# Two 128-step chunks in place of the third 256-step window, and a new order of all work, in an RWKV recurrence followed by an MLP mixer

## The chip, the cores and the metric

The kernel runs on one core of a Trainium2 chip. Its engines work side by side, each through its own list of instructions: TensorE (PE) multiplies matrices, VectorE (DVE), ScalarE (ACT) and GpSimd (POOL) work elementwise, and SyncE (SP) issues transfers; POOL and ACT issue some too. The metric is the device time of one execution in microseconds (us). Several runs of the kernel before give its median.

## The reference

Inputs are r, k, v of 4 batches x 8 heads x 768 steps x 48, a decay w and a bonus u of 8 heads x 48, and four mixer weights, all f32. Per head, a 48x48 state runs over the steps:

```python
for t in range(S):
    cur = np.einsum('bhd,bhe->bhde', u[None] * kt, vt)
    y[:, :, t] = np.einsum('bhd,bhde->bhe', rt, state + cur)
    state = w[None, :, :, None] * state + np.einsum('bhd,bhe->bhde', kt, vt)
```

So each output has a part from the state of earlier steps and a part from its own step, `cur`. The outputs, as x of 4 x 768 x 384, go through a mixer: `u = x + (relu(x^T w_tok1) w_tok2)^T`, over the 768 steps with 256 hidden, and `out = u + relu(u w_ch1) w_ch2`, over the 384 columns with 1536 hidden.

## The kernel before

**Chunks and windows.** A batch's 768 steps are six chunks of 128. In an ordinary chunk (`unit`, from line 801) k and r of 128 steps x 384 columns are scaled by powers of the decay (`kr`), transposed by PE (`tr_ps` or `trk`, copied to SBUF as `rkb`, `rka`), and multiplied head by head into 128x128 scores (`at_ps`); DVE masks these to earlier steps (`AT0` and `AT1`, for the even and the odd heads); PE multiplies the masked scores by v and adds the state's part (`y_ps`). The state is carried from chunk to chunk: key-value products (`kv_ps`), masked and decayed to `S0`. For the own step, the product of k, r and u is summed over a head (`pr`, `ad_ps`, `adg`) and weighs v (`yd`).

Batch 0 is worked in *windows* of 256 steps (`window`, from line 527; its loads and products `pairs`, from line 626). One load then brings two neighbouring steps to each partition (`win`, 384 KB, against 192 KB of a chunk's `kt`, `rt`, `vt`). Even and odd steps are worked apart, so a window has two sets of scores of 64x128 for each half, masked by `mask2`, and outputs of 32 small matmuls (`y_ps<-vb,AT`, line 750). Its own-step part, `ydb`, is put in place by four PE matmuls against `place` (line 760), and the sum leaves PSUM by a plain copy into `x_b0`. `two_steps` (line 451) says which loads are windows. r of an ordinary chunk in batches 0 and 1 is loaded for two chunks at once as well.

**The mixer.** `h_ps` (x by `wtok1`; batch 0 in three groups: chunks 0 to 2, then 3 and 4, then 5), relu to `h1r`, then back by `wtok2` (`hx_ps`, `hT_ps`) to `u_sb`, transposed to `uT`; `z_ps` (up by `wch`, 12 blocks), relu to `zr`, `h_ps` (down by `wch`), plus u into `osb`, and stores.

**What sets the order.** All work is cut into tasks with names; `Plan.run` (lines 151 to 198) emits them in the sequence of the table ORDER. Each engine runs its own tasks in that sequence, and waits for what they need. BUFS says which buffer each tile takes, ENGINES which engine does a task that several could do. WAITS (line 130) ties a few transfers to the start of an earlier one. The weights are fetched by POOL, in its list between its products (`load_weights`, line 501): `wtok1`, `wtok2`, two parts of `wch1`, and three of `wch2`. FILL puts matmuls on a constant tile (`warm`) ahead of some tasks, with results that nobody reads; NWARM more of them are tasks of their own (`keep_warm`, line 1209).

All engine calls go through a helper, so nearly all rows of the profile have one line, L239; they are told apart by tiles.

Of the kernel before, what the change touches and what calls it, by code (L numbers as in the profile page):

```python
# [21 lines left out]
    0, 3, 7, 22, 2, 19, 17, 51, 1, 38, 42, 5, 21, 52, 4, 12, 6, 867, 868, 23, 20, 54, 15, 55, 24, 8, 18, 9, 16, 45,  # L22
    27, 58, 29, 120, 28, 13, 43, 118, 30, 53, 14, 121, 10, 149, 57, 869, 870, 871, 872, 873, 874, 875, 876, 877, 878,
    123, 119, 150, 879, 122, 124, 147, 56, 25, 44, 152, 125, 46, 148, 177, 61, 26, 126, 132, 36, 153, 135, 11, 39,
    134, 127, 151, 129, 41, 59, 178, 136, 133, 154, 140, 181, 179, 141, 60, 161, 184, 155, 143, 180, 128, 162, 156,
    164, 158, 70, 144, 111, 182, 157, 137, 169, 183, 131, 166, 138, 63, 37, 163, 130, 194, 145, 165, 112, 170, 139,
    185, 167, 159, 188, 173, 195, 160, 175, 146, 196, 171, 34, 191, 113, 174, 168, 142, 186, 192, 172, 199, 187, 193,
    49, 189, 205, 31, 190, 200, 197, 114, 176, 201, 40, 198, 203, 202, 310, 204, 33, 206, 306, 210, 207, 219, 312,
    208, 209, 307, 213, 216, 313, 225, 211, 32, 220, 217, 221, 222, 62, 214, 218, 318, 223, 212, 215, 66, 226, 224,
    308, 65, 227, 228, 309, 252, 234, 253, 314, 256, 235, 68, 320, 258, 116, 232, 259, 115, 240, 64, 229, 233, 260,  # L30
    241, 238, 261, 71, 250, 321, 236, 377, 268, 322, 237, 230, 269, 339, 323, 257, 246, 340, 231, 274, 311, 324, 247,
    73, 315, 264, 316, 239, 275, 317, 262, 265, 251, 341, 343, 266, 117, 342, 326, 267, 329, 327, 50, 270, 67, 351,
    263, 345, 328, 272, 333, 254, 346, 242, 330, 271, 353, 273, 319, 69, 244, 243, 347, 331, 325, 334, 335, 348, 276,
    354, 349, 332, 248, 355, 245, 337, 249, 277, 78, 48, 373, 359, 255, 74, 35, 281, 374, 366, 47, 278, 367, 385, 84,
    282, 279, 75, 301, 336, 344, 360, 356, 72, 362, 283, 357, 302, 284, 375, 363, 76, 512, 387, 376, 296, 361, 82,
    379, 388, 303, 352, 380, 386, 77, 338, 389, 368, 297, 381, 369, 79, 393, 350, 370, 382, 298, 394, 383, 358, 88,
    304, 378, 401, 371, 502, 384, 364, 280, 395, 396, 80, 286, 372, 510, 291, 397, 299, 81, 507, 390, 398, 400, 391,
    503, 292, 85, 365, 392, 402, 399, 521, 539, 287, 403, 87, 522, 404, 515, 285, 513, 516, 293, 406, 405, 90, 407,
    417, 294, 531, 413, 421, 418, 410, 414, 536, 508, 411, 415, 408, 412, 511, 288, 541, 409, 91, 419, 544, 424, 420,
    527, 86, 442, 514, 542, 528, 422, 432, 537, 289, 428, 504, 433, 434, 443, 429, 430, 425, 505, 83, 435, 426, 431,  # L40
    518, 568, 427, 545, 438, 525, 562, 440, 439, 519, 446, 441, 423, 506, 560, 436, 482, 437, 540, 563, 92, 444, 447,
    483, 445, 416, 573, 526, 472, 532, 520, 509, 550, 529, 551, 570, 547, 564, 484, 543, 533, 548, 473, 89, 554, 534,
    448, 574, 555, 474, 449, 565, 535, 462, 523, 463, 477, 571, 566, 524, 546, 466, 549, 517, 478, 93, 572, 552, 538,
    95, 530, 556, 454, 485, 99, 479, 553, 455, 475, 467, 470, 96, 569, 480, 452, 561, 557, 575, 576, 453, 97, 471,
    456, 567, 584, 450, 94, 578, 682, 464, 451, 577, 558, 98, 579, 583, 458, 581, 580, 105, 468, 684, 457, 582, 585,
    459, 559, 487, 305, 692, 469, 586, 465, 460, 295, 683, 690, 587, 461, 102, 687, 488, 685, 588, 688, 589, 492, 691,
    695, 590, 701, 592, 591, 702, 693, 594, 696, 593, 597, 707, 595, 601, 711, 489, 596, 497, 490, 493, 598, 103, 740,
    686, 498, 100, 602, 599, 713, 494, 600, 719, 698, 603, 495, 604, 700, 689, 499, 605, 705, 106, 721, 626, 108, 699,
    610, 694, 290, 716, 618, 706, 703, 622, 619, 724, 628, 623, 608, 629, 714, 616, 725, 500, 614, 609, 646, 617, 745,
    717, 638, 715, 647, 709, 708, 615, 697, 624, 639, 104, 627, 620, 750, 109, 625, 611, 640, 710, 621, 101, 632, 748,  # L50
    704, 641, 634, 633, 606, 742, 635, 727, 607, 491, 722, 644, 735, 746, 650, 645, 734, 612, 753, 723, 642, 729, 652,
    751, 754, 712, 728, 630, 643, 730, 743, 752, 636, 631, 107, 731, 720, 657, 110, 718, 651, 637, 732, 613, 744, 496,
    648, 726, 736, 658, 649, 486, 737, 756, 481, 733, 653, 741, 764, 672, 747, 757, 476, 738, 758, 300, 759, 677, 749,
    763, 654, 760, 755, 761, 739, 765, 762, 659, 766, 678, 660, 767, 661, 673, 768, 769, 667, 770, 772, 771, 774, 679,
    773, 775, 777, 779, 776, 778, 662, 680, 781, 663, 681, 782, 501, 668, 674, 780, 664, 655, 783, 784, 665, 669, 785,
# [1200 lines left out]
```

## Time and profile before

| | |
|---|---|
| device time, median of 3 runs | 160.15 us (160.04 to 160.2) |
| span of the profiled execution | 158.2 us (its own device time is not given; the median is 1.95 above the span) |
| PE busy | 151.8 us, 96%, 1574 matmuls |
| DVE busy | 107.0 us, 68% |
| ACT busy | 77.7 us, 49% |
| POOL busy | 90.1 us, 57% |
| moved by DMA | 27.39 MB, mean 173 GB/s |

The busy time of PE is modelled from pipelined matmuls. The page, the tables by stretches, the chain of waits and the timeline are shown in the prediction, where each is used. In timelines, a row is: start, busy time, engine, line, operation, written tile <- read tiles, form, count, and in brackets the idle time ahead and what ended it. `L239` becomes `L242` in the changed kernel, since the tables are longer.

### The profile page before, as it was taken

How to read it: one execution, taken by the hardware profiler on the slowest of the kernel's cores; microseconds unless marked ns; L12 is line 12 of the kernel's file. 1: busy time of each engine (PE TensorE's matmuls, PEld its weight loads, DVE VectorE, ACT ScalarE, POOL GpSimd, SP SyncE). 2: the span in 40 equal slices, each digit the busy share in tenths (PEclk: the TensorE clock that was granted, in tenths of full speed). 3: DMA queues.
4: the chain of work that ended last, by engine and by line, in shares of the span. 5: the costliest groups of instructions: out<-in, count | busy, mean ns of one | idle time of the engine just before them, and what ended most of it. 6: DMA issues, size and time to landing. Idle time of an engine off the chain costs nothing.

```text
span 158.2 us, 4001 instructions
## 1 busy us (share of the span) xinstructions
PE 151.8 (96%) x1574; PEld 101.3 (64%) x1574; DVE 107.0 (68%) x218; ACT 77.7 (49%) x187; POOL 90.1 (57%) x120
## 2 busy tenths in 40 slices
PE   6988999999999999999999999999999999999991
PEld 1356767776767676666677665576666566666660
DVE  2689992468967994467989637898987465432071
ACT  3677797737990581478476440235643102463000
POOL 7859969444183799999928999398920000000000
PEclk9999999999999999999999999999999999999999
DMA  4999999999989999999999989999992075300044
GB/s 125 265 261 264 205 204 210 229 204 210 227 176 187 203 230 195 187 210 136 220 194 173 227 158 129 190 193 215 145 274 101 29 176 146 126 0 4 0 151 147
DMA packets 88148, 27.39 MB, mean 173 GB/s; under 512 B 82753, under 2 KB 87234, under 8 KB 88130
## 3 DMA queue, kind: packets, MB, share of 16 engines
q1 hardware_dynamic: 85776, 23.86, 76.1%
q0 software_dynamic: 2160, 3.15, 11.7%
q8 instruction: 12, 0.20, 0.5%
q10 hardware_dynamic: 194, 0.14, 0.3%
q14 instruction: 6, 0.05, 0.1%
HBM read 20.65 MB, written 4.72 MB: 160 GB/s over the span
## 4 chain that ended last, share of the span: by engine, by line
PE 87%; DVE 4%; DMA 3%; POOL 2%; ACT 1%; issue 1%; POOLq 0%; ACTq 0%
PE h_ps L239 35%; PE z_ps L239 29%; PE y_ps L239 6%; PE at_ps L239 4%; PE kv_ps L239 3%; PE hT_ps L239 3%; PE hx_ps L239 3%; DVE kr L239 3%; DMA uT<-u_sb 3%; PE tr_ps L239 2%; PE ad_ps L239 1%; PE trk L239 1%; POOL mask L239 1%; ACT rka L239 1%; POOL bm L239 1%
## 5 line engine op out<-in xcount | busy, mean ns | idle before, releaser
L239 PE MATMUL h_ps<-wch,zr 128*128 128x384 bf16 (+2 forms) x300 | 53.4, 319 | 0.0
L239 PE MATMUL z_ps<-uT,wch 128*128 128x384 bf16 x288 | 52.4, 327 | 0.3 <-DMA uT<-u_sb 0.3
L239 ACT ACTIVATE zr<-z_ps 128x384 bf16<-128x384 f32 x63 | 28.7, 492 | 36.1 <-PE z_ps L239 35.9
L239 PEld LDWEIGHTS <-wch 128*128 128x128 bf16 x288 | 31.1, 114 | 13.4 <-DMA uT<-u_sb 0.7
L239 PEld LDWEIGHTS <-zr 128*128 128x128 bf16 x300 | 27.6, 98 | 15.7
L239 DVE TENSOR_TENSOR AT<-at_ps,mask 128x512 bf16<-128x512 f32 x48 | 30.6, 682 | 2.2 <-PE at_ps L239 2.2
L239 DVE TENSOR_SCALAR zr<-z_ps 128x384 bf16<-128x384 f32 x33 | 17.7, 554 | 13.5 <-PE z_ps L239 13.5
L239 POOL TENSOR_TENSOR yd<-vb,adg 128x384 f32<-128x384 bf16 x13 | 10.6, 829 | 10.8 <-ACT vb L239 5.9
L239 DVE TENSOR_TENSOR osb<-u_sb,h_ps 128x384 f32<-128x384 bf16 (+2 forms) x19 | 10.0, 531 | 9.6 <-PE h_ps L239 9.0
L239 PEld LDWEIGHTS <-kr 128*128 128x128 bf16 (+1 forms) x196 | 11.6, 97 | 3.9 <-DVE kr L239 0.7
L239 POOL TENSOR_TENSOR kr<-rt,wp 128x384 bf16<-128x384 f32 x12 | 12.0, 1005 | 3.1 <-DMA rt<-in_r_dram 3.1
L239 POOL TENSOR_TENSOR ku<-kw,u_bc 128x384 f32<-128x384 f32 x12 | 11.9, 1003 | 2.4 <-DMA u_bc<-in_u_dram 2.4
L239 DVE TENSOR_TENSOR u_sb<-x_b,hT_ps 128x384 bf16<-128x384 bf16 x15 | 7.9, 550 | 6.5 <-PE hT_ps L239 6.4
L239 POOL TENSOR_TENSOR rku<-ku,rt 128x384 f32<-128x384 f32 x12 | 12.0, 1002 | 0.2
L239 POOL TENSOR_TENSOR kr<-kw,wnat 128x384 bf16<-128x384 f32 x12 | 12.0, 1004 | 0.0
L239 ACT CAST vb<-vt 128x384 bf16<-128x384 f32 x18 | 9.0, 513 | 2.5 <-DMA vt<-in_v_dram 2.5
L239 PEld LDWEIGHTS <-wtok 128*128 128x128 bf16 x78 | 7.3, 98 | 4.1
L239 DVE TENSOR_TENSOR x_b<-y_ps,yd 128x384 bf16<-128x384 f32 x18 | 9.4, 551 | 0.6 <-PE y_ps L239 0.5
L239 ACT ACTIVATE yd<-vb,adg 128x48 f32<-128x48 bf16 x40 | 9.5, 322 | 0.1
L239 ACT COPY rkb<-tr_ps 128x1024 bf16<-128x1024 bf16 x6 | 6.1, 1013 | 6.7 <-PE tr_ps L239 6.7
L239 PE MATMUL h_ps<-x_b,wtok 128*128 128x384 bf16 x48 | 8.8, 326 | 0.0
L239 PE MATMUL y_ps<-vb,AT 128*128 128x48 bf16 (+1 forms) x240 | 8.4, 182 | 0.0
(99 smaller groups left out, 190.8 us busy)
## 6 DMA issues: line engine op xcount, KB each, us to landing
out_dram<-osb SPq DMA_DIRECT2D x23, 192.0 KB, 2.6
vt<-in_v_dram SPq DMA_DIRECT2D x18, 192.0 KB, 3.5
win<-in_r_dram SPq DMA_DIRECT2D x6, 384.0 KB, 6.2
kw<-in_k_dram SPq DMA_DIRECT2D x12, 192.0 KB, 4.6
rt<-in_r_dram SPq DMA_DIRECT2D x12, 192.0 KB, 4.0
wch<-in_moe_w_ch_dram POOLq DMA_DIRECT2D x4, 384.0 KB, 6.4
win<-in_k_dram SPq DMA_DIRECT2D x3, 384.0 KB, 5.7
win<-in_v_dram SPq DMA_DIRECT2D x3, 384.0 KB, 7.1
```

The costliest lines, as they stand in the source:

```text
L239: return lambda *args, **kw: tc.keep_in_program_order(f(*args, **kw))
```

## The change

The third window of batch 0 (chunks 4 and 5) isn't a window any more: `PAIRED` loses it. Its k and v come as chunks of 128 steps, its scores are masked by the ordinary `mask`, and its outputs are 12 matmuls for each chunk. `PE_ADDS` is emptied: it says for which ordinary chunks of batch 0 PE adds the own-step part, and before there were none. So chunks 4 and 5 add it when DVE evicts `y_ps` (`result`, line 974). `FILL` loses seven matmuls. ORDER, BUFS and ENGINES are new throughout; all else in the code is the same.

```diff
 ORDER = [
-    0, 3, 7, 22, 2, 19, 17, 51, 1, 38, 42, 5, 21, 52, 4, 12, 6, 867, 868, 23, 20, 54, 15, 55, 24, 8, 18, 9, 16, 45,
...
+    3, 1, 7, 45, 10, 20, 23, 17, 8, 0, 885, 874, 883, 4, 2, 18, 51, 12, 16, 5, 38, 52, 877, 13, 55, 882, 6, 19, 54,
...
-FILL = {132: 3, 140: 3, 206: 1, 879: 1}
+FILL = {879: 1}
-PAIRED = [(0, 0), (0, 1), (0, 2)]
+PAIRED = [(0,0),(0,1)]
...
-PE_ADDS = [0, 1, 2, 3, 4, 5]
+PE_ADDS = []
```

**POOL's list ahead of the first weights.** Before, from its first product to the second weight load (`kr..` are scaled k or r from a load `win..` or `kt..`; `wGm2` is the decayed mask of the state; `ydb..` is an own-step part):

```order
L239 TENSOR_TENSOR kr2_69<-win_135,wnpair_89 128x8x48
L239 TENSOR_TENSOR kr4_71<-win_154,wpair_88 128x8x48
L239 TENSOR_TENSOR wGm2_94<-bm_93,wG2_91 128x384
L239 TENSOR_TENSOR kr4_71<-win_154,wpair_88 128x8x48
L239 TENSOR_TENSOR kr5_72<-win_172,wnpair_89 128x8x48 x2
L239 DMA wtok1_100<-in_moe_w_tok1_dram 128x6x256
L239 TENSOR_TENSOR ydb_431<-vb2_300,adg2_368 128x384
L239 TENSOR_TENSOR ydb_474<-vb2_300,adg2_368 128x384
L239 DMA wtok2_101<-in_moe_w_tok2_dram 128x1536
```

and now, from the product of the second window's k:

```order
L242 TENSOR_TENSOR kr3_70<-win_150,wnpair_89 128x8x48 x2
L242 TENSOR_TENSOR wGm2_94<-bm_93,wG2_91 128x384
L242 TENSOR_TENSOR ydb_321<-vb2_291,adg2_289 128x384
L242 TENSOR_TENSOR ydb_375<-vb2_291,adg2_289 128x384
L242 TENSOR_TENSOR kr5_72<-kt_190,wnat2_84 128x8x48
L242 MEMSET mask_80 128x128
L242 AFFINE_SELECT mask_80<-mask_80 128x128
L242 TENSOR_TENSOR kr0_67<-kt_223,wnat2_84 128x8x48
L242 DMA wtok1_100<-in_moe_w_tok1_dram 128x6x256
L242 TENSOR_TENSOR kr2_69<-win_550,wpair_88 128x8x48 x2
L242 DMA wtok2_101<-in_moe_w_tok2_dram 128x1536
L242 TENSOR_TENSOR yd_653<-vb_570,adg_589 128x384
```

Both own-step products of the first window and the making of `mask` now stand ahead of the load of `wtok1`, and two products of batch 1 (`win_550`) between it and `wtok2`.

**DVE's list up to the outputs of the last chunks of batch 0.** Before, with the third window's masks last:

```order
L239 TENSOR_TENSOR AT0_498<-at_ps_381,mask2_81 128x512
L239 TENSOR_TENSOR pr2_507<-tr_ps_324,rka2_429 128x1024
L239 TENSOR_TENSOR AT0_555<-at_ps_476,mask2_81 128x512
L239 TENSOR_TENSOR AT1_564<-at_ps_477,mask2_81 128x512
L239 TENSOR_TENSOR S0_590<-kv_ps_419,wGm2_94 128x384
L239 TENSOR_TENSOR AT0_606<-at_ps_571,mask2_81 128x512
L239 TENSOR_TENSOR AT1_621<-at_ps_572,mask2_81 128x512
L239 TENSOR_TENSOR ydb_636<-vb2_545,adg2_619 128x384
L239 CAST x_b0_98<-y_ps_641 128x384
```

and now, with the masks of chunk 4 (`AT1_564`, `AT0_566`) and then of chunk 5:

```order
L242 COPY adg2_469<-ad_ps_460 128x16
L242 TENSOR_TENSOR ydb_471<-vb2_391,adg2_469 128x384
L242 TENSOR_TENSOR S0_487<-kv_ps_430,wGm2_94 128x384
L242 TENSOR_TENSOR pr_537<-trk_423,rkb_454 128x512
L242 TENSOR_TENSOR ydb_543<-vb2_391,adg2_469 128x384
L242 TENSOR_TENSOR pr_548<-trk_473,rkb_454 128x512
L242 TENSOR_TENSOR AT1_564<-at_ps_555,mask_80 128x512
L242 TENSOR_TENSOR AT0_566<-at_ps_554,mask_80 128x512
L242 TENSOR_TENSOR AT1_634<-at_ps_524,mask_80 128x512
L242 TENSOR_TENSOR AT0_638<-at_ps_523,mask_80 128x512
L242 TENSOR_TENSOR x_b0_98<-y_ps_608,yd_653 128x384
L242 TENSOR_TENSOR x_b0_98<-y_ps_640,yd_665 128x384
```

The second window's two own-step products are both on DVE now, ahead of the masks, and the eviction of chunks 4 and 5 reads `yd` as a second operand where it was a cast.

More of the change, by code (lines that the diff above doesn't have):

```diff
@@ L95 @@
     'l': [
-    0, 1, 2, 3, 4, 5, 6, 7, 8, 9, 10, 11, 0, 2, 1, 3, 4, 5, 6, 7, 8, 9, 10, 11, 1, 3, 5, 6, 0, 8, 9, 2, 4, 7, 10, 11,
+    0, 1, 2, 3, 4, 5, 6, 7, 8, 9, 10, 11, 0, 1, 2, 3, 4, 5, 6, 7, 8, 9, 11, 10, 0, 1, 2, 4, 3, 5, 11, 8, 6, 9, 0, 1,
+    2, 7, 10, 4,
     ],
     'g': [
-    0, 1, 2, 3, 4, 5, 0, 1, 2, 4, 3, 5, 0, 1, 2, 3, 0, 4, 1, 2, 5,
+    0, 1, 2, 3, 4, 5, 0, 1, 2, 3, 4, 5, 1, 0, 2, 3, 4, 0, 1, 5, 3, 2,
     ],
@@ L104 @@
     'v': [
-    0, 1, 2, 3, 4, 5, 6, 1, 0, 2, 3, 4, 5, 6, 1, 2, 0, 4, 3, 5, 6, 2, 1, 4,
+    0, 1, 2, 3, 4, 5, 6, 0, 1, 2, 3, 4, 5, 6, 0, 1, 2, 3, 4, 5, 6, 1, 2, 0,
     ],
     'u': [
-    0, 1, 2, 3, 4, 5, 6, 7, 1, 0, 2, 5, 4, 3,
+    0, 1, 2, 3, 4, 5, 6, 7, 0, 1, 4, 2, 3, 5,
     ],
     'zr': [
-    0, 1, 2, 1, 0, 2, 1, 0,
+    0, 1, 2, 1, 0, 1, 2, 0,
     ],
```

16 lines of the change are left out of this document (8 added, 8 removed), and 106 rows, old and new, of tables (BUFS, ENGINES, ORDER).

## The prediction

> **What bounds the kernel now.** I read the profile's page first, then the table by stretches of the span, then the chain of waits, and last the timeline of the first 32 us.
>
> ```profile
> span 158.2 us, 4001 instructions
> PE 151.8 (96%) x1574; PEld 101.3 (64%) x1574; DVE 107.0 (68%) x218; ACT 77.7 (49%) x187; POOL 90.1 (57%) x120
> PE   6988999999999999999999999999999999999991
> PE 87%; DVE 4%; DMA 3%; POOL 2%; ACT 1%; issue 1%; POOLq 0%; ACTq 0%
> L239 PE MATMUL z_ps<-uT,wch 128*128 128x384 bf16 x288 | 52.4, 327 | 0.3 <-DMA uT<-u_sb 0.3
> ```
>
> (The second row is busy time by engine, the third the busy tenths of PE in 40 slices, the fourth the chain that ended last, the fifth a group with the idle time ahead of it and what ended that.) TensorE's matmuls are 96% of the span and 87% of the chain. After the first three slices PE is full to the end, so 1 us of matmuls removed is worth 1 us only where nothing else makes PE wait instead.
>
> ```profile
> 0.00:10.00 10.00, 8.17 (x34) 3.29 (x34) 5.87 (x16) 4.95 (x8) 7.69 (x30) 1.00 0.96 208
> 10.00:20.00 10.00, 9.27 (x238) 6.83 (x239) 9.42 (x20) 7.97 (x15) 9.25 (x11) 1.00 1.27 239
> 20.00:30.00 10.00, 10.00 (x160) 6.89 (x154) 6.53 (x12) 8.38 (x20) 7.53 (x9) 1.00 1.16 206
> ```
>
> (Columns: the stretch, its length, busy us of PE, PEld, DVE, ACT, POOL, then granted clock, DMA share, GB/s.) From 20 us on PE has no gap in that stretch; later it waits 0.3 us once for `uT`, a transfer, by the group's row above. From 0 to 20 us it is short of work by 1.83 + 0.73 us: there the loads, DVE (9.42 of 10) and POOL (9.25) decide. So the question is when the seam from the ramp to the full stretch comes, and how much PE work lies behind it.
>
> ```profile
> 22.54 1.08 PE h_ps L239 x6
> 23.62 1.49 PE y_ps L239 x44
> 25.12 0.81 PE h_ps L239 x5
> 29.43 0.45 PE tr_ps L239 x8
> 44.87 0.37 PE y_ps L239 x12
> 45.24 0.65 PE h_ps L239 x4
> 154.72 0.42 DVE osb L239
> ```
>
> (Rows of the chain: start us, length, work.) The seam is at 22.54, the first `h_ps` group: six matmuls of chunks 0 to 2 by `wtok1`. From there the chain is PE's own list, one task behind another, up to 154.72.
>
> **The change part by part.** The sum goes from the seam: its new start, plus the change in PE's list behind it, plus new waits behind it, plus the tail.
>
> *PE's list behind the seam.* Before, the outputs of the third window of batch 0 stand behind it, 1.49 us in the chain (44 matmuls). Now chunk 4's ordinary output stands ahead of it and chunk 5's behind: 0.37 by the row at 44.87, an ordinary chunk's 12 matmuls. The filling matmul inside the next `h_ps` group goes: that group is 0.81 against 0.65 for the same four matmuls at 45.24, so 0.16. The transposes of batch 1's first window (0.45, the row at 29.43) now stand ahead of the seam, in the wait there. Sum: 1.49 + 0.16 + 0.45 - 0.37 = **1.73 us less**. The rest of PE's list has the same tasks in another order, costed at nothing; if orders that put forms with 64 and 128 rows in other neighbourhoods cost 0.1 to 0.2 us for some few switches, it is 0.4 either way.
>
> The six filling matmuls in the ramp (three at 10.86, three at the first key-value products) also go:
>
> ```profile
> 2.22 1.64 PE L239 MATMUL w_ps<-wp,ones 1*128 1x384 f32 x2
> 3.80 4.06 PE L239 MATMUL kv_ps<-warm 128*128 128x512 bf16 x10
> 6.57 0.28 POOL L239 MEMSET mask<- 128x128 f32 x1
> 6.92 0.41 POOL L239 TENSOR_SCALAR_AFFINE_SELECT mask<-mask 128x128 f32<-128x128 f32 x1
> 7.76 1.30 POOL L239 TENSOR_TENSOR kr<-win,wnpair 128x384 bf16<-128x384 f32 x1 [0.18 <-DMA win<-in_k_dram]
> 8.35 1.01 ACT L239 COPY rka<-tr_ps 128x1024 bf16<-128x1024 bf16 x1 [1.12 <-PE tr_ps L239]
> 9.97 1.01 ACT L239 COPY rkb<-tr_ps 128x1024 bf16<-128x1024 bf16 x1 [0.61 <-PE tr_ps L239]
> 10.86 0.81 PE L239 MATMUL at_ps<-warm 128*128 128x512 bf16 x3
> 11.60 0.64 PE L239 MATMUL at_ps<-rkb,rka 64*64 64x128 bf16 x32
> 11.66 1.14 POOL L239 TENSOR_TENSOR wGm<-bm,wG 128x384 f32<-128x384 f32 x1
> 12.14 0.69 DVE L239 TENSOR_TENSOR pr<-tr_ps,rka 128x1024 bf16<-128x1024 bf16 x1
> 13.63 1.23 DVE L239 TENSOR_TENSOR AT<-at_ps,mask 128x512 bf16<-128x512 f32 x2
> 15.63 1.03 POOL L239 DMA_DIRECT2D wtok<-in_moe_w_tok_dram  x1
> 16.68 1.63 POOL L239 TENSOR_TENSOR ydb<-vb,adg 128x384 bf16<-128x384 bf16 x2
> 21.00 0.62 ACT L239 ACTIVATE wnat<-lnw,iota 128x384 f32<-128x384 f32 x1
> 22.82 0.95 DVE L239 TENSOR_TENSOR ydb<-vb,adg 128x384 bf16<-128x384 bf16 x1
> ```
>
> (Timeline: start, busy us, engine, line, operation, tiles, count.) They stand in PE's gaps of the ramp (8.17 of 10 there), so on the path I cost them at 0; at most 0.81, the length of the first three, which the scores at 11.60 follow.
>
> *The masks, one of the two things that the seam waits for.* The first scores come at about 10.2 instead of 11.60: no fillers stand ahead of them, and of the two 1.01 us copies of transposed keys and receptances (8.35 and 9.97, both on ACT) one is now on DVE. From there DVE's list up to chunk 4's second mask has: two 1024-wide products at 0.69, ten masks at 0.62 (1.23 for two), two products into `kr` and two into `ydb` and two into `S0` at 0.55, two 512-wide products at half of 0.69, a copy of 0.17. That is 1.4 + 6.2 + 3.3 + 0.7 + 0.2 = 11.8: masks at 22.0.
>
> ```profile
> L239 DVE TENSOR_TENSOR kr<-win,wpair x6: 546/553/1347, 6.6 to 36.6; 128x384 bf16<-128x384 f32 x6
> L239 POOL TENSOR_TENSOR kr<-win,wpair x6: 992/1000/1014, 10.7 to 46.3; 128x384 bf16<-128x384 f32 x6
> L239 DVE TENSOR_TENSOR osb<-u_sb,h_ps x19: 289/553/555, 81.5 to 154.7; 128x384 f32<-128x384 bf16 x17, 128x128 f32<-128x128 bf16 x1, 128x256 f32<-128x256 bf16 x1
> ```
>
> (One tile's groups: minimum, median and maximum in ns.) A DVE product of two SBUF operands takes 0.55 us, but 1.35 where POOL's product lies beside it (POOL's own takes 1.00); `ydb` took 0.95. With 4 such products in the long form it is 22.0 + 2 x 0.8 + 2 x 0.4 = 24.4; and 21.0 where ACT's and PE's part runs 1 us ahead. I take 22.3, nearer to the short form because POOL's work is spread over all of this time as before. Chunk 4's outputs add 0.37: 22.7.
>
> *The first weights, the other.* `wtok1` is issued by POOL in its own list, before at 15.63. Its list ahead of that issue is longer now. The third load that POOL waits for, k of window 1, is now fourth:
>
> ```profile
> 6.00:9.00 3.00, 2.96 (x20) 1.46 (x18) 3.00 (x6) 1.88 (x4) 2.74 (x7) 1.00 1.28 262
> 9.00:12.00 3.00, 2.47 (x47) 1.80 (x51) 2.40 (x5) 2.32 (x6) 1.36 (x3) 1.00 1.27 261
> 21.00:24.00 3.00, 3.00 (x75) 1.76 (x63) 2.77 (x5) 2.96 (x9) 1.71 (x3) 1.00 1.10 198
> win<-in_r_dram SPq DMA_DIRECT2D x6, 384.0 KB, 6.2
> wtok<-in_moe_w_tok_dram POOLq DMA_DIRECT2D x2, 384.0 KB, 6.3
> wch<-in_moe_w_ch_dram POOLq DMA_DIRECT2D x1, 768.0 KB, 8.3
> ```
>
> The stretches again, then three groups of transfers (KB each, median us to landing). At 262 GB/s a window load of 384 KB takes 393,216 / 262,000 = 1.50 us, and POOL's product at 7.76 began on that load's landing; so now at 7.76 + 1.50 = 9.2. Behind it: two products of 1.00 (11.2); `wGm2`, which needs ACT's `wG` (POOL began it at 11.66, so 11.7 again) 1.00 (12.7); two `ydb` 1.63 (14.3); a product 1.00; the mask for ordinary chunks, 0.28 + 0.41, which stood at 6.57 before; another product 1.00: 17.0. Up to 1.2 of waiting beside DVE's products comes on top; I take 17.5, as POOL's rows held 1.00 in nearly all cases. The landing takes 6.3 (the `wtok` row): **23.8**. It is 23.0 if POOL is done by 16.7, 24.8 if at 18.2 and the transfer takes a little longer beside the smaller loads. At 23.75 against 22.7 for the masks the weights end last. The seam goes from 22.54 to 23.75, **1.2 later** (0.5 to 2.3).
>
> *What is late next.* `wtok2`, `wch1` (two parts) follow on POOL, with two products of batch 1 and both `yd` of chunks 4 and 5 between them. With 1.03 for an issue (the row at 15.63), 1.00 for a product and 0.82 for a `yd`, they go at 17.5 + 3.0 = 20.5, 23.2 and 24.2. The first two land 6.3 later at 26.8 and 29.5; the last is twice as large, 8.3 by its own row: 32.5, or 33.5 if it queues. PE's list needs them 3.6, 6.5 and 10.4 us behind the seam, by the rows of its tasks: 27.3, 30.2, 34.1. So 0.5, 0.7 and 0.6 to 1.6 us of slack. The third window's k and v now come as loads of one chunk, and are issued well ahead of their use. Further small waits: DVE's product for batch 1 ahead of the first relu, its scores, and `uT` of batch 2, with 4.4 us of PE work to cover it where 4.6 did. Together **0.2** (0 to 0.7).
>
> *Own step and tail.* For chunks 4 and 5 PE's placing matmuls (4 of 384 columns) are replaced by an addition in DVE's eviction, which ran as a copy. DVE has 0.23 free of 3 us at 21:24, so it may cost up to the difference of a product and a cast, 0.1, once; covered by `h_ps` matmuls of chunks 0 to 2 (1.08). The order of the last pieces turns: the final addition is 128 columns wide instead of 256. The third row of the tile's groups has 0.289 as its minimum, the 128-column piece, against 0.42 at the chain's end: **0.13 less**.
>
> **Sum.** -1.73 + 1.2 + 0.2 - 0.13 = -0.46 us. The profiled span is 158.2, so 157.7; the runs' device time lies 160.15 - 158.2 = 1.95 above it, and so 159.7 us. My bounds of the terms together give 159.2 to 160.2 for this case.
>
> **The rivals.**
>
> *B, the weights come earlier.* If POOL's products aren't held up (16.7) and the landing is as short as the window loads' 6.2, `wtok1` is there at 23.0 and the masks at 22.3 + 0.37 aren't much sooner: seam + 0.45, no waits behind it. -1.73 + 0.45 - 0.13 = -1.4: 158.8. For it: PE's first gap is shorter, since the scores come 1.4 us sooner. Against: two products that stood behind the issue now stand ahead of it.
>
> *C, slower: the chain of weights becomes the bound.* If POOL gets `wG` or the second window's `adg` late (ACT has the two `wnat` activations, 0.62 each at 21.00 before, ahead of its first copy now), the issue goes to 18.5, landing 24.8; since all weights go through one queue, 2 us late on the first is 2 us late on `wtok2` and `wch1`, whose slack is 0.5 to 0.7. PE then waits 2.2 at the seam and another 0.7 to 1.3 at the back and up groups. -1.73 + 2.2 + 1.0 - 0.13 = +1.35 (up to 2): about 161.0 with some more of it at the masks. It decides from a POOL issue of some 18.0. For it: in before POOL and DVE were already full in 10:20. Against: before, PE never waited for the weights' landing.
>
> *D, slower: the clock.* The granted clock is 1.00 in every stretch, though PE stood 0.53 us in the stretch from 9 to 12. The ten `warm` matmuls at 3.80 took 0.41 each and the three at 10.86 0.27 each, so the rate does rise during the ramp. PE's first work now is the `w_ps` group, which ran at 2.22, and the `warm` matmuls come behind it instead of ahead; and with seven fillers fewer the gap ahead of chunk 4's outputs is 1 to 1.5 us. If the rise comes 1 us later, 1 us of work takes double: +0.5; if it falls back in that gap for 3 us, +1.5. 159.7 + 2.0 is about 161.5. By the Trainium skill ("TensorE: Matmul & The Clock Gate", section "Part 1: The HAM clock gate (the "warmup" mystery)") a throttled clock is the default, and is released after a free-running window of about 3.4 us of sustained activity, and closes after an idle one; the trace agrees with the first half, and no stretch here shows the second. By that rule a gap under its window costs nothing.
>
> *That the change doesn't do what it says* is out: with the third window worked by chunks its 40 matmuls are gone from PE's list.
>
> **How the numbers follow.** Chances: A 0.45, B 0.22, C 0.25, D 0.08. What a measurement can tell from no change is 0.2%, 0.32 us: 159.83 to 160.47. A lies at 159.7, just beyond it; of its 0.45 I put 0.24 as faster, 0.17 as the same, 0.04 slower. B is faster (0.22); C slower 0.22, the same 0.03; D slower. Faster 0.46, same 0.20, slower 0.34. The range of 8 in 10 goes from B's 158.8 less 0.2 to C's 161.0 plus 0.3: 158.6 to 161.3.
>
> **What would show it.** `h_ps` of chunks 0 to 2 begins at 23.4 to 24.1, and what ends the wait ahead of it is the DMA of `wtok`: A. At 22.9 to 23.2 it is B; after 24.5, with waits of `hx_ps` or `z_ps` for weights, C. If a mask ends the wait, my order of the two is wrong. POOL's issue of `wtok1` at 17.5 and PE's list behind the seam 1.73 us shorter are the two terms of the sum to look at; a granted clock below 1.00 or `warm` matmuls at over 0.4 us past 8.5 us would be D. What would make it wrong: waits of PE in the full stretch, 30 to 150 us, of over 0.7 us.

## The result, and the profile after

The changed kernel takes 164.9 us (median of 4 runs, 164.46 to 167.02) against 160.18 for the kernel before on the same chip: ratio 1.0286, interval 1.0265 to 1.0307. It is slower, and outside the range that was forecast. The ratios leave out executions over 1.5% slower than the kernel's fastest, as the one of 167.02 us here. The page of the changed kernel (span, busy time by engine, busy tenths of PE, chain, one group):

```profile
span 163.2 us, 3905 instructions
PE 151.7 (93%) x1527; PEld 101.2 (62%) x1527; DVE 110.8 (68%) x224; ACT 76.9 (47%) x190; POOL 87.8 (54%) x115
PE   4998889999999999999979989998999997999992
PE 55%; DMA 26%; POOL 8%; DVE 3%; SPq 3%; issue 2%; ACT 2%; POOLq 0%
L242 PE MATMUL z_ps<-uT,wch 128*128 128x384 bf16 x288 | 51.6, 327 | 1.4 <-DMA uT<-u_sb 1.4
```

PE's row has digits below 9 far behind the ramp, and the chain, 87% PE before, is now 26% transfers. The table of PE's waits says for what (total us, times, longest):

```profile
PE at_ps L242 <- DMA rk<-kr: 1.8, 2, 1.1
PE z_ps L242 <- DMA uT<-u_sb: 1.4, 2, 1.1
PE kv_ps L242 <- DVE S L242: 0.8, 1, 0.8
PE y_ps L242 <- DVE AT L242: 0.6, 1, 0.6
PE h_ps L242 <- DMA wtok<-in_moe_w_tok_dram: 0.2, 1, 0.2
```

Scores (`at_ps`) wait for `rk`, the transposed keys and receptances of batches 2 and 3, which DMA transposes; `z_ps` waits for `uT`, another such transpose. The chain of the changed kernel gives the places (start, length, work):

```profile
17.62 6.99 DMA wtok<-in_moe_w_tok_dram
24.66 1.15 PE h_ps L242 x6
...
78.44 5.00 DMA rk<-kr
83.48 0.62 PE at_ps L242 x16
...
97.88 3.87 DMA uT<-u_sb
...
110.26 3.58 DMA rk<-kr
113.88 0.62 PE at_ps L242 x16
...
130.92 4.82 DMA uT<-u_sb
...
160.09 0.29 DVE osb L242
```

Four transposes, two of `rk` and two of `uT`, now stand on the path, where one of `uT` stood before (at 98.17). The stretches of the changed kernel, in the columns of the prediction:

```profile
15.00:18.00 3.00, 2.23 (x55) 1.29 (x44) 3.00 (x6) 1.76 (x3) 2.93 (x5) 1.00 1.11 209
21.00:24.00 3.00, 2.33 (x39) 1.54 (x37) 3.00 (x8) 1.53 (x7) 0.47 (x2) 1.00 1.31 220
80.00:90.00 10.00, 8.86 (x115) 6.34 (x114) 7.53 (x16) 5.16 (x15) 7.70 (x9) 1.00 1.27 221
130.00:140.00 10.00, 8.93 (x55) 5.55 (x54) 4.81 (x10) 0.49 (x1) 0.00 (x0) 1.00 0.55 100
```

In the ramp DVE is full (3.00 of 3) while PE has 2.23 and 2.33; from 80 to 90 and from 130 to 140 PE lacks 1.1 us each, where it lacked nothing before.

**An account that adds up.** I give each PE task the usual interval of its form in the kernel before, and call the sum "PE's list". Up to the first scores of batch 2 (the first `at_ps<-rk`, at 69.89 before and 68.09 after) the time above the list is the *front share*; from there to the end of the span it is the *rest share*, with the tail in it. All these figures are of one profiled execution of each kernel.

```
                     before   after   change
PE's list from seam  129.37   128.05   -1.32
front share           23.51    26.14   +2.63   (69.89 - 46.38; 68.09 - 41.95)
rest share             5.27     8.99   +3.72
span                 158.15   163.18   +5.03
```

Counted by tiles as well as forms, or by pairs of neighbouring forms, the list's change comes out between -1.0 and -1.5. In the front share the seam is 2.1 (22.54 to 24.66, by the rows of the chains). The rest share holds single waits at 82.3 (1.34), 94.4 (0.57), 101.4 (0.55), 113.3 (0.81) and 134.7 (1.26), where before had one of some 0.5.

### The profile page after: what moved, and what is told of

It reads as the page before. It is cut to its first block, busy times and chain, and to the rows that moved or that the text cites. A ratio compares the mean times of both kernels' runs of the same rounds, so it can differ in the third digit from the quotient of the medians.

```text
span 163.2 us, 3905 instructions
## 1 busy us (share of the span) xinstructions
PE 151.7 (93%) x1527; PEld 101.2 (62%) x1527; DVE 110.8 (68%) x224; ACT 76.9 (47%) x190; POOL 87.8 (54%) x115
## 4 chain that ended last, share of the span: by engine, by line
PE 55%; DMA 26%; POOL 8%; DVE 3%; SPq 3%; issue 2%; ACT 2%; POOLq 0%
PE h_ps L242 20%; PE z_ps L242 19%; DMA vt<-in_v_dram 5%; DMA uT<-u_sb 5%; DMA rk<-kr 5%; DMA rt<-in_r_dram 5%; DMA wtok<-in_moe_w_tok_dram 4%; POOL kr L242 4%; PE kv_ps L242 4%; SPq L242 3%; PE y_ps L242 2%; PE hT_ps L242 2%; PE hx_ps L242 2%; PE at_ps L242 2%; PE tr_ps L242 2%; POOL rku L242 2%
## 5 line engine op out<-in xcount | busy, mean ns | idle before, releaser
L242 PE MATMUL z_ps<-uT,wch 128*128 128x384 bf16 x288 | 51.6, 327 | 1.4 <-DMA uT<-u_sb 1.4
L242 ACT ACTIVATE zr<-z_ps 128x384 bf16<-128x384 f32 x66 | 29.7, 492 | 40.3 <-PE z_ps L242 40.0
L242 DVE TENSOR_SCALAR zr<-z_ps 128x384 bf16<-128x384 f32 x30 | 16.0, 552 | 9.8 <-PE z_ps L242 9.8
L242 POOL TENSOR_TENSOR yd<-vb,adg 128x384 f32<-128x384 bf16 x14 | 11.6, 830 | 13.0 <-DVE adg L242 4.5
L242 DVE TENSOR_TENSOR x_b<-y_ps,yd 128x384 bf16<-128x384 f32 x20 | 10.5, 552 | 2.0 <-PE y_ps L242 1.8
L242 POOL TENSOR_TENSOR kr<-kt,wnat 128x384 bf16<-128x384 f32 x5 | 5.3, 1067 | 8.2 <-DMA kt<-in_k_dram 8.2
```

Source lines behind the costliest of these rows:

```text
L242: return lambda *args, **kw: tc.keep_in_program_order(f(*args, **kw))
```

## Which part of the order: first four runs

The theories, by the names of the expectations: T1, late weights on POOL's queue; T2, the new order behind the seam; T3, the loads of single chunks, which would take more of the transfer engines; T4, below.

One thing is not held the same in these runs. e1, e2, e5, e6, e8, e12 and e13 keep the BUFS of the kernel that they start from. e3, e4, e7, e9 to e11 and e14 to e17 have another order, and with it a BUFS made anew: of the 252 or 254 entries that place tiles in PSUM, where matmuls write, 187 to 221 differ from that kernel's. The fences show the order alone. What the other table does is seen in the section on the rest.

**e1**: the loads of `wch1` and the first of `wch2` are put ahead of the own-step products of chunks 4 and 5 (one number of ORDER to a row).

```diff
 209
+115
+116
+117
 190
...
 321
-115
 258
...
-116
...
-117
```

> The changed kernel with three numbers moved in its ORDER: the loads of both parts of wch1 and the first part of wch2 stand on POOL ahead of the own-step products of chunks 4 and 5, for whose sums POOL waited 2.53 us. They should issue at about 21.2 to 23 instead of 25.3 to 26.9. Theory T1 (late weights hold back SP's queue, whose loads of batches 1 and 2 wait for their landing, and so POOL's products and the transposes of batches 2 and 3): of the waits behind the seam two thirds or more go, 161 to 163 us. Theory T2 (the new order of the work of batches 1 to 3 has these waits in itself, whenever the weights come): 164 to 165. Theory T3 (the loads of single chunks take more of the transfer engines, and set all behind them back): 164 to 165.

164.41 us, ratio 1.0223 (1.0152 to 1.0295). The rest still waits: 0.89 at 101.3, 1.41 at 113.4, 0.91 at 135.4. But the median mixes two things: the two executions with the granted clock at 1.00 took 162.83 and 163.58 us, against 164.46 to 164.92 of the change's with 0.999 or more; the other two, with the clock at 0.99 and 0.979, took 165.23 and 166.92. So with the clock held the weights' place may be worth some 1.5 us. No run tests this with more executions or a held clock.

**e2**: no load of batches 1 and 2 is tied to a weight any more.

```diff
-WAITS = {(0, 2, 2): [(0, 0, 0)], (0, 4, 0): [(0, 2, 0)], (0, 4, 2): [(0, 0, 2)], (1, 0, 1): [(0, 2, 0)], (1, 0, 2):
-    [2], (1, 1, 0): [(0, 2, 2)], (1, 1, 2): [3], (1, 2, 0): [(0, 4, 1)], (1, 2, 1): [(0, 2, 2)], (1, 2, 2): [(0, 4,
-    2)], (1, 3, 0): [1], (1, 3, 2): [(0, 2, 2)], (1, 4, 0): [(0, 4, 1)], (1, 4, 1): [(0, 4, 1)], (1, 4, 2): [0], (1,
-    5, 0): [(0, 2, 0)], (2, 0, 0): [4], (2, 0, 1): [5], (2, 0, 2): [3], (2, 1, 0): [4], (2, 1, 2): [5], (2, 2, 0):
-    [3], (2, 2, 2): [4], 2: [(1, 0, 1)], 3: [(0, 4, 0)], 4: [(1, 0, 1)], 5: [(0, 4, 2)], 6: [(0, 2, 1)]}
+WAITS = {(0, 2, 2): [(0, 0, 0)], (0, 4, 0): [(0, 2, 0)], (0, 4, 2): [(0, 0, 2)], (1, 0, 1): [(0, 2, 0)], (1, 1, 0): [(0, 2, 2)], (1, 2, 0): [(0, 4, 1)], (1, 2, 1): [(0, 2, 2)], (1, 2, 2): [(0, 4, 2)], (1, 3, 2): [(0, 2, 2)], (1, 4, 0): [(0, 4, 1)], (1, 4, 1): [(0, 4, 1)], (1, 5, 0): [(0, 2, 0)], 2: [(1, 0, 1)], 3: [(0, 4, 0)], 4: [(1, 0, 1)], 5: [(0, 4, 2)], 6: [(0, 2, 1)]}
```

> The changed kernel without the entries of WAITS that make loads of batches 1 and 2 wait for the landing of a weight; the ties of loads to loads and of weights to loads stay. SP no longer stands 10.8 us behind wch. T1: the loads of batch 1 start some 8 us sooner, the waits behind the seam shrink by 2 us or more: 161 to 163 us, less if weights land later for the company. T2: no gain, 164 to 165. T3: no gain, 164 to 165.

165.11 us, 1.0304 (1.0271 to 1.0337); waits of 1.7 at 100.9, 0.55 at 113.7, 0.89 at 134.9.

**e3** takes the changed kernel up to the seam and then the order of before; **e4** is the opposite, the kernel before up to the seam and then the order of the change.

```diff
 197
-212
-216
 205
 210
-213
-225
+873
 62
...
```

and, for e4 against the kernel before,

```diff
 205
-31
 190
 200
 197
-114
 176
 201
-40
 198
 203
+202
+204
+31
...
```

> The change of the first batch alone: all tasks up to the first h_ps group, and chunks 4 and 5, in the changed kernel's order and on its engines; all others in the order and on the engines of the kernel before. Buffers are given to the one free longest. wch1 stays behind the own-step products of chunks 4 and 5, as in the changed kernel. T2: the seam is 2.1 us later, the list behind it 1.73 shorter, nearly no waits: 160 to 161 us. T1: the weights are as late as in the changed kernel, so the waits stay: 163 to 165. T3: 163 to 165.

> The reverse: the first batch in windows and in the order of the kernel before, up to the first h_ps group and the third window's outputs; all other tasks in the changed kernel's order and on its engines. T2: the waits of batches 2 and 3 come with that order: 163 to 165 us. T1: wch1 is issued at 20 to 25 as before, so most waits are gone: 160 to 162. T3: no loads of single chunks, 160 to 161.

e3 takes 163.0 us, 1.0151 (1.0107 to 1.0194); e4 takes 165.24, 1.0301 (1.0277 to 1.0325). From e4's page and its table of waits:

```profile
span 163.0 us, 3990 instructions
PE z_ps L245 <- DMA uT<-u_sb: 1.4, 1, 1.4
PE z_ps L245 <- ACT zr L245: 0.6, 1, 0.6
PE z_ps L245 <- DVE AT L245: 0.6, 1, 0.6
```

e4's seam is at 22.62 (22.54 before), it works the third window the old way, and it is as slow as the whole change. So the rest's new order, with its engines and buffers, is enough to make the kernel slow: T2 stands. T3 falls as the cause, since e4 has no loads of single chunks in place of the window. T1 falls as the whole cause, since neither the place of the weights (e1) nor the ties (e2) remove the waits; the 1.5 us of e1 stay open. How much of e4's loss is the sequence of tasks isn't shown: some 2.4 us of its waits stand at places where the change has none, and look like the work of its own BUFS (below). e3 takes 1.5% more than before with the old rest behind the new front, its own BUFS included.

## Instruction fetches beside the transposes (T4)

The page lists a small queue, `q8 instruction: 12, 0.20, 0.5%`: twelve fetches of 16 KB. In the changed kernel's transfer records they start at 78.0, 90.8, 107.3, 119.1, 133.5 and so on, about every 250 PE instructions. The `uT` issued at 130.92 took 4.82 us to land, and its packets stand still from 133.5 to 135; the `rk` issued at 75.33 took 5.72. Over before, after and e1 to e4, transposes in whose time a fetch started took 4.73 us in the median (24 of them), those without 3.55 (53). (A long transpose also has more time for a fetch to start in, so the medians alone don't show which is the cause.) To move the fetches without moving any work, the filling matmuls at the start are split in parts, so that every later PE instruction stands further on in the program: 52 rows in **e5** (the change), **e7** (e3) and **e8** (before), 12 in **e6** (the change, a control).

```diff
-    def keep_warm(cols):
+    def keep_warm(cols, parts):
...
-                pe.matmul(bank[0][:, 512 - cols:512], warm[:, 0:128], warm[:, 0:cols], start=fresh or cols == 512, stop=True,
-                          skip_group_check=True)
+                for p in range(parts):
+                    lo, hi = cols * p // parts, cols * (p + 1) // parts
+                    pe.matmul(bank[0][:, 512 - cols + lo:512 - cols + hi], warm[:, 0:128], warm[:, lo:hi],
+                              start=fresh or cols == 512, stop=True, skip_group_check=True)
...
-        add("PE", "warm", keep_warm(512 if i in WIDE_AT else 128), [t_warm])
+        add("PE", "warm", keep_warm(512 if i in WIDE_AT else 128, 3 if i < 13 else 1), [t_warm])
```

(e6 has `3 if i < 3`.)

> The changed kernel with each warm matmul issued as three of a third of its columns (the same columns in all): some 52 more instructions ahead on PE, nothing else moved. In the trace's transfer records the queue for instructions fetches 16 KB about every 245 PE instructions, in the changed kernel at 78.0, 107.3 and 133.5 us, each time while a transpose by DMA (rk, uT) is under way, and such transposes take 4.7 us in the median against 3.5 without a fetch. With 52 rows more the fetches should come at about 75.9, 103.4 and 129.5, outside the last two. Theory T4 (these fetches make the transposes late): the wait for uT at 134.7 (1.3 us) goes and those for rk at 82 and 113 shrink: 162 to 163.6 us. Theory T2 (the new order makes them late, whatever is fetched): 164.5 to 165.5.

> The same with three of the warm matmuls split: 12 more instructions. The fetches come about 1 us sooner (77.5, 106.4, 132.6) and stay inside the same transposes. T4 and T2: as the changed kernel, 164.4 to 165.5, with the waits at 82, 113 and 134 still there.

> The new front with the old rest (163.0 us), with the warm matmuls split as above: 52 more instructions ahead. There the fetch at 131.3 lay in both uT transposes (4.8 and 4.4 us) and PE waited 1.07 us at 132.7. T4: the fetch comes at about 127, the wait goes, 161.6 to 162.3 us. T2: 162.7 to 163.3.

> The kernel before with the warm matmuls split in the same way. Its fetches move from 71.4, 95.5 and 112.1 to about 69, 92 and 109, beside rk transposes, and from 121.7 and 142.6 to 119 and 138, clear of uT. The split itself should cost nothing. T4: 160.1 to 161.2, as far as these rk have slack. T2: 160.0 to 160.5.

e8: 160.45, 1.0001 (0.9978 to 1.0024), so the splitting costs no more than the noise. e5: 164.08, 1.0245 (1.0191 to 1.03), 0.8 us less than the change by the medians, though the intervals overlap. Its waits:

```profile
PE z_ps L242 <- DMA uT<-u_sb: 1.8, 2, 1.6
PE at_ps L242 <- DVE pr L242: 0.9, 1, 0.9
PE at_ps L242 <- DMA rk<-kr: 0.2, 1, 0.2
```

The wait at 134.7 is gone and those for `rk` are down from 1.8 to 0.2, but `uT` is now waited for 1.7 us from 100.3 to 102.1. The fetch at 104.0 comes behind that wait and can't be its cause; e13 below, whose fetch is at 104.5, has the same wait (1.69). e6 took 165.39, from 162.06 to 166.39, too wide a spread for a ratio; its waits stay. In e7, 163.83 (1.0208, 1.0175 to 1.0241), the wait for `uT` at 132.7 is gone, but the clock fell for a time in every execution (0.987), so its time says nothing. T4 holds for single waits (those at 134.7 and 132.7). A gain in the whole time isn't clear of the noise.

## The clock

In e1 the stretches show a granted clock below 1.00 behind the ramp:

```profile
21.00:24.00 3.00, 1.65 (x28) 1.11 (x28) 3.00 (x7) 0.69 (x3) 2.59 (x4) 1.00 1.29 176
24.00:27.00 3.00, 2.42 (x24) 1.61 (x22) 1.87 (x4) 2.34 (x6) 1.65 (x2) 0.52 1.18 249
27.00:30.00 3.00, 3.00 (x39) 2.27 (x38) 1.77 (x4) 0.49 (x1) 0.00 (x0) 0.91 1.18 206
```

PE had 1.65 us of work in the stretch ahead, and from 24.1 to 27.6 (3.41 us) it ran at half the clock, so that up to 1.7 us of its time was lost. e2, e7, e9 and e10 show the same, and one execution each of the change (167.02 us) and of e12. **e13** is the change with ten filling matmuls, put into the ramp's gaps; **e12** is the kernel before without its seven.

```diff
-FILL = {879: 1}
+FILL = {879: 1, 140: 3, 171: 5, 169: 2}
```

```diff
-FILL = {132: 3, 140: 3, 206: 1, 879: 1}
+FILL = {879: 1}
```

> The kernel before with FILL as in the change, without its seven filling matmuls and with nothing else changed. Theory D (they hold the clock): the granted clock falls to half for 3.4 us in some executions, 161 to 162 us, and a wider spread. If they only fill gaps: 159.9 to 160.4 us, 0.16 us less on the path.

> The changed kernel with the same ten filling matmuls in PE's gaps from 14 to 20 us. Theory D: none of its executions has a granted clock under 0.99 any more, and the median stays or falls a little, 164.0 to 164.9 us, since most of its executions held the clock without them. If the fillers lie on the path: 165.3 us or more.

e12: 160.72, 1.0041 (1.0011 to 1.0071). e13: 164.42, 1.0264 (1.0239 to 1.0289), clock 0.999 or more in all four executions. So the change is as slow with the clock held: the clock is not what the median lost. That the fillers hold it is likely and not sure: one execution in four lost it without them (one in ten of e12), none of e13's, but three of six of e15 (below), which has the same fillers, show 0.99.

## The front: weights or masks

S1 says that the seam waits for `wtok1`, S2 that it waits for PE's and DVE's own chain of scores and masks. **e9** puts `wtok1` (113) behind the first window's own-step products, `wtok2` (114) behind chunk 4's k product, a product of batch 1 (314) later, and the second window's own-step products on POOL. **e14** is e9 with e13's fillers.

```diff
 132
+113
 165
...
 183
+114
 182
...
-113
...
-114
...
-314
 196
 211
+314
```

> The changed kernel with its front set otherwise: wtok1 is issued behind POOL's first two own-step products (at about 15 instead of 17.6), wtok2 behind the last product for chunk 4; the two own-step products of the second window are POOL's again and not DVE's; the transposes of batch 1's first window come behind the first h_ps group. All behind it stays. Theory S1 (the late seam is those lists: wtok1's place and DVE's products, which take 0.55 to 2.4 us beside POOL's): the first h_ps group starts at 22.6 to 23.3 instead of 24.7, 163.0 to 163.8 us. Theory S2 (the masks of single chunks set the seam): it starts at 24 or later, 164.3 to 165.2.

> The changed kernel with the mended front and the ten filling matmuls, its own order behind. S1 with D: the clock stays, the seam comes at 22.8 to 23.5 instead of 24.7, 163.2 to 164.2 us. S2: 164.4 us or more.

e9: 167.0, 1.0444 (1.0407 to 1.0482), with the clock fallen. e14: 165.74, 1.0362 (1.0324 to 1.04), clock 1.00. From e14's timeline:

```profile
14.29 1.03 POOL L246 DMA_DIRECT2D wtok<-in_moe_w_tok_dram  x1
17.89 0.97 PE L246 MATMUL kv_ps<-warm 128*128 128x384 bf16 x5 [1.09 <-DVE S L246]
23.40 2.48 DVE L246 TENSOR_TENSOR AT<-at_ps,mask 128x512 bf16<-128x512 f32 x4 [0.82 <-PE at_ps L246]
```

`wtok1` is issued 3.3 us sooner and landed at 21.2, and yet the seam is at 25.11: the masks of chunks 4 and 5 begin only at 23.40. So S1 falls here, and S2 stands: the masks set this seam. Part of their lateness is the run's own: PE waited 1.1 for the state and then ran the five fillers of the second row, so that its next task began at 18.70, where the change has it at 17.67. In e9, without fillers, the masks begin at 23.43, but the clock was halved from 19.5 to 23.0. In the changed kernel both ended nearly together:

```profile
19.60 1.47 DVE L242 TENSOR_TENSOR ydb<-vb,adg 128x384 bf16<-128x384 bf16 x1
21.79 0.54 DVE L242 TENSOR_TENSOR ydb<-vb,adg 128x384 bf16<-128x384 bf16 x1
22.59 2.47 DVE L242 TENSOR_TENSOR AT<-at_ps,mask 128x512 bf16<-128x512 f32 x4
```

Chunk 4's two masks end at 22.59 + 2.47/2 = 23.8, its outputs follow until 24.4, and `wtok1` lands at 24.6: the 0.2 that `h_ps` waits for it.

**e10** is e9's front without the two products of batch 1, with `wch1` and the second decayed state mask (37, 40) ahead of the own-step products, and the old rest; the `warm` matmuls at the start are split in four. **e11** is e10 with 37 and 40 put back and e13's fillers.

```diff
 209
+115
+116
+37
+40
 190
```

```diff
 115
 116
-37
-40
 190
...
-FILL = {879: 1}
+FILL = {879: 1, 140: 3, 171: 5, 169: 2}
```

> That front, chunks 4 and 5 as the change has them, and behind it the order and engines of the kernel before; both parts of wch1 and the second decayed mask stand on POOL ahead of the own-step products of chunks 4 and 5; the warm matmuls are split in four, so that instructions are fetched at about the same places of the tail as before. If the time was lost in the lists and not in the change of form (S1 and T2 with T4): seam at 23, list 1.5 us shorter, waits under 1.5 us, 158.8 to 160.3 us. If chunks in place of the window cost it (S2 or T3): 161.5 us or more.

> The front of the run before with the old rest, and two things mended that its trace showed: the second decayed mask stands again behind the own-step products of chunks 4 and 5 (POOL waited 3.1 us in front of them), and ten filling matmuls stand in PE's gaps from 14 to 20 us (three, five and two), where the granted clock fell to half at 20 to 23.4. Theory D (gaps of PE before the seam let the clock fall): granted clock 1.00 throughout, seam at 22.8 to 23.4, 159.8 to 160.8 us. If the clock falls all the same, or the seam is set by the chunks' masks (S2): 161.5 us or more.

e10: 163.59, 1.0207 (1.0183 to 1.023), clock down to 0.977. e11: 161.89, 1.0106 (1.0077 to 1.0134), the best version with chunks in place of the window:

```profile
span 160.7 us, 4024 instructions
PE kv_ps L246 <- DVE S L246: 1.1, 1, 1.1
PE trk L246 <- POOL kr L246: 1.0, 1, 1.0
```

No transfer is waited for behind the seam any more; the front share is 72.81 - 45.73 = 27.1, and the rest share 4.9, less than before (5.27). So in the three kernels with a new front and the old rest (e3, e10, e11) the front costs more than the shorter list gives.

## The rest: four places, or late as a whole

Why does PE wait in the new rest? Here are the last scores of batch 3 and the transposes ahead of them in the changed kernel, from its timelines,

```profile
107.94 1.58 SPq L242 DMA_TRANSPOSE rk<-kr  x1
110.26 1.59 SPq L242 DMA_TRANSPOSE rk<-kr  x1
113.88 0.62 PE L242 MATMUL at_ps<-rk 64*128 64x128 bf16 x16 [0.61 <-DMA rk<-kr]
```

and in the kernel before:

```profile
109.03 4.66 SPq L239 DMA_TRANSPOSE rk<-kr  x2
115.59 0.62 PE L239 MATMUL at_ps<-rk 64*128 64x128 bf16 x16
```

The second of that pair was issued at 111.3. So the preparation (loads, POOL's products, SP's list) ends only 1 us sooner, but PE's list from the seam to these scores is 83.3 us instead of 90.5: PE asks 2.4 us sooner (113.27 against 115.66), and stands. At all six scores of batches 2 and 3, from the last issue to the end of PE's work ahead of the scores, before had 4.2 to 6.7 us, the change 3.0 to 4.8, for transposes of:

```profile
DMA to landing us min/median/max: 3.2/4.0/5.7
```

(The tile's table for the changed kernel; 3.1/3.4/4.9 before.)

**e15** is e13 with PE tasks put behind ready ones: the scores 582 (the wait at 82) behind 1.14 us, 733 behind 1.46, the first `z_ps` of batches 2 and 3 behind 0.65 each. 733 turned out not to be the scores with the wait at 113; those are 762. **e16** is e13 with 762 behind 2.13 us, and **e17** has 582, 762 and both `z_ps`.

```diff
 572
-582
 469
...
 476
+582
+583
...
 654
-733
-735
...
 618
+733
+735
+740
+741
```

```diff
 721
-762
-770
 642
...
 624
-673
 614
 625
+762
+764
+763
+770
+769
+673
 678
```

> The changed kernel with ten matmuls on the constant tile in the front (as in the run of that kind before: 164.42 us), and in the rest of its order four PE tasks are put behind ready ones: the scores of chunks 4 and 5 of batch 2 behind one group of h_ps and one of z_ps (0.65 + 0.49 us of PE work), the scores of chunks 2 and 3 of batch 3 behind three groups of z_ps (1.46 us), the first z_ps of batch 2 behind one group of h_ps (0.65), and the first z_ps of batch 3 behind one (0.65), their masks and relus with them. In that run PE stood 0.41, 1.2, 1.72 and 0.64 us at these four places. L (the new order asks for transposed keys and states too soon behind their issue: 3.0 to 4.75 us, against 4.2 to 6.7 before, where the transposes take 3.2 to 5.7): the added cover takes 0.4 + 1.2 + 0.65 + 0.64 = 2.9 us of the waits away, the masks come later but their outputs have room, and the time is 161.5 to 162.3. Q (the rest is held back as a whole, by loads, POOL's products and SP's list, and PE's waits are only where that shows): the waits come back at the outputs y_ps, at kv_ps or at the next scores, and the time is over 163.6.

> The changed kernel with ten matmuls on the constant tile in the front (164.42 us so), and the last scores of batch 3 (chunks 4 and 5; the run before moved the ones ahead of them in their place) put behind four groups of z_ps and one of kv_ps: 2.13 us of PE work goes ahead of them, the masks follow. F (the preparation is done at its own time: the last transposes were issued at 110.3 to 111.1 us in all runs of the new rest and land some 3.7 later; behind the last scores PE has 44.7 us of list, against 38.9 before, and the end follows from the two): the transposes are issued at 110.3 again, the 1.2 us that PE stood ahead of these scores is gone, the list behind is 42.6, and the time is 163.2 (162.9 to 163.5). Q (whatever is filled comes back elsewhere): a like wait comes at the outputs of chunk 4 or at the first z_ps of batch 3, and the time stays at 164.2 or more.

> The last but one edit with the last scores in place of the wrong ones: the scores of chunks 4 and 5 of batch 2, the first z_ps of batch 2 and of batch 3 behind ready PE work (0.4, 0.65 and 0.64 us of waits), and the last scores behind 2.13 us. The run with the first three stood 2.36 us ahead of the last scores with their transposes issued at 110.99, and took 165.02 to 165.16 us in its executions with the clock at 1.00. F: of the 2.36 us 2.13 go, and the time is 163.0 (162.7 to 163.4), no more than 0.3 under the run of this call that moves the last scores alone, since the last transposes come at the same time in both. L (four places, each with its own wait): 161.9 to 162.3, some 1.2 under the other run. Q: 164.5 or more.

e15: 166.65, 1.0394 (1.0348 to 1.0439; 165.02 to 166.84, in part with the clock at 0.99). e16: 164.94, 1.0285 (1.0234 to 1.0336). e17: 164.44, 1.0269 (1.0247 to 1.029). None beats e13's 164.42. But in e17 the waits for `rk` and `uT` in the rest are nearly gone:

```profile
110.83 0.47 PE L246 MATMUL at_ps<-rk 64*128 64x128 bf16 x8 [0.26 <-DMA rk<-kr]
111.51 3.69 PE L246 MATMUL z_ps<-uT,wch 128*128 128x384 bf16 x21 [0.21 <-DVE AT L246]
139.72 6.01 PE L246 MATMUL z_ps<-uT,wch 128*128 128x384 bf16 x36 [0.58 <-ACT zr L246]
```

The account says where it went (us; the scores are the first of batch 2):

```
                before  after   e4     e11    e13    e14    e15    e16    e17
scores start     69.89  68.09  68.75  72.81  67.96  69.88  69.01  69.61  69.84
front share      23.5   26.1   25.5   27.1   26.0   27.9   27.1   27.7   27.9
rest share        5.3    9.0    8.1    4.9    8.7    8.0    8.3    7.6    7.1
```

Moving the four tasks takes 1.7 us off the rest share (8.74 to 7.05). Of that, 0.7 comes without the moves in e14, which has the old places and comes as late; some 1.0 is left for them. The whole 1.7 was lost again ahead of the scores: e15 to e17 have e13's order there, and yet a front share 1.1 to 1.9 larger. The timelines show where. The first two rows are e13's, the other two e17's:

```profile
27.72 0.85 PE L242 MATMUL hx_ps<-ident,x_b 128*128 128x128 bf16 x12
30.75 0.62 PE L242 MATMUL at_ps<-rkb,rka 64*128 64x128 bf16 x16
29.32 0.34 PE L246 MATMUL hx_ps<-ident,x_b 128*128 128x128 bf16 x3 [0.26 <-DVE pr L246]
32.41 0.38 PE L246 MATMUL at_ps<-rkb,rka 64*128 64x128 bf16 x7 [0.19 <-ACT uT L246]
```

e17 stops within these runs of matmuls, and what ends the stops (`pr`, `uT`) are tiles that these matmuls don't read. DVE's `pr` and ACT's `uT` read PSUM, though: the reading that fits is that in the other BUFS the matmul's tile takes a PSUM buffer that they have yet to empty. The same stops, counted against the usual interval, come in e15, e16 and e17 alike: 0.42 at `hx_ps`, 0.41 at `at_ps`, 0.26 at the first `z_ps`, 1.1 us ahead of the scores, and 0.38 at `at_ps` (77 to 78) and 0.74 at `z_ps` (140) behind them. e4, e9 and e14 have most of them too. The change, e1, e2, e5, e6 and e13, which share one BUFS, have none. The rest of the 1.9 is the seam, at 24.82 to 25.36 against e13's 24.77.

So e15 to e17 changed two things, and their times decide nothing between L, F and Q: Q's time came, but not by its mechanism, since the waits for transposes did not come back in the rest; by the stops alone e17 lost 1.1 us ahead of the scores that e13 did not. The moves with the old BUFS, or the other BUFS without the moves, were not run.

## Why the prediction was wrong, by its steps

**PE's list** was to be 1.73 us shorter, and is 1.32 by forms, 1.5 with the shorter switches between forms. Right in kind, 0.2 to 0.4 too large.

**The seam** was to come 1.2 later (0.5 to 2.3), and came 2.1 later. POOL issued `wtok1` at 17.62, where 17.5 was forecast; the landing took 6.99 instead of 6.3. The masks of chunk 4 were to be done at 22.3 and were at 23.8: the first scores came at 10.89 and not at 10.2, and DVE's products beside POOL's were long (1.15 and 1.47 us) more often than I took, so that the long form, 24.4, was the nearer one. So both terms were mis-sized, inside their ranges. The weights did end last, but by 0.2 us and not by 1.05, so that sooner weights alone would have gained next to nothing.

**"The rest of PE's list has the same tasks in another order, costed at nothing"** is the step that failed, together with "further small waits, 0.2 (0 to 0.7)". Waits behind the seam are about 5 us instead of 0.5, over 3 of them for transposes of `rk` and `uT`, and the rest share grew by 3.7; with the old rest behind the new front (e11) that share is 4.9 again. e4 has the new rest behind the old front and is as slow as the whole, with the reserve made above. The prediction named its test itself, waits of over 0.7 us from 30 to 150. What was missing was a comparison that the two lists and the trace of before allowed: how much PE work stands ahead of each task that waits for a transfer, in the old list and in the new, against the slack in the old trace. At the last scores the new list had 7.2 us less of it, where before the transposes, issued at 111.3 and 3.4 us under way by the median, were there about 1 us ahead of their use at 115.66. That this shortage of cover makes the waits is read from the trace; the runs that were to show it (e15 to e17) have the other BUFS.

**The tail** was to be 0.13 shorter, and was 0.35.

**The rivals.** C had the sign, but by another mechanism: no weight was late but `wtok1`, and `hx_ps` and `z_ps` never waited for one. Its sum was also set too low: +1.35 on 160.15 is 161.5, not 161.0, which would have put the top of the range at 161.8, still short of the result. D's mechanism is real in single executions and takes up to 1.7 us of PE's time there, but e13 shows that the median does not rest on it. B didn't come. *That it doesn't do what it says* was rightly out.

**What stays open**: which part of the preparation (loads that wait for a buffer, POOL's products, SP's list) holds the transposes of batch 3 at 110.3 to 111.6 in the runs of the new rest; whether the sequence of tasks, the engines or the buffers of the new rest make its waits; what e1's place of the weights gives with the clock held; and why single executions of one kernel differ so much (e6: 162.06 to 166.39).

## What to carry to other kernels

When an order is made anew, cost nothing at zero because "the tasks are the same": for every task that waits for a transfer, compare the work ahead of it on its engine in both lists, and hold the difference against the slack that the old trace shows. A kernel whose main engine never waits may have 1 us of slack at dozens of places, and fewer instructions bring each of them nearer. And a wait that is filled gives its time back only if the engine comes on time to the place: account for the front and the rest apart. Where a run has another order, look whether the table of buffers has changed with it, and give that table a run of its own.

## What the hardware showed that I had not expected

- **Fetches of instructions delay transposes.** In the change the packets of a `uT` under way stand still from 133.5 to 135, with a fetch at 133.5; with the fetches moved by 52 rows of program the wait for it is gone (e5), as is the like one of e3 (e7).
- **The clock falls for one window though PE isn't idle.** In the 3.41 us ahead of the fall PE was busy 1.86 us in e1, 2.28 in e2, 1.90 in e7, 1.98 in e9 and 2.19 in e10, and then the clock was halved for 3.41 us. With fillers in those gaps it stayed at 0.999 or more in e11, e13 and e14, but not in e15. The Trainium skill ("TensorE: Matmul & The Clock Gate", section "Part 1: The HAM clock gate (the "warmup" mystery)") speaks of a free-running window of about 3.4 us and of an idle one that closes the gate; the length agrees with the 3.41 us here, but the stretch ahead was 54 to 67% busy, not idle.
- **A DVE product beside POOL's has no one price.** The same own-step product took 0.69 us in e3, 1.47 in the change, 2.17 in e2 and 2.39 in e1.
- **The first weights' landing has no one price either.** 5.71 us in e3, 6.99 in the change, 7.7 in e1 and e2. A load of 384 KB was issued some 1 us behind them in the last three and none in e3, but e14 took 6.87 with one that was issued only 0.4 us ahead of the landing, so that this isn't all of it.
